# Decode attention plus gated MLP on one core: K turned by VectorE in 32x32 blocks instead of by TensorE

## The chip, the cores and the metric

One core of a Trainium2 chip runs the whole kernel. The time is that of one execution on the device, in microseconds (us); less is better. Engines: PE (TensorE) multiplies matrices and writes PSUM, DVE (VectorE) and ACT (ScalarE) work elementwise, POOL (GpSimd) fills constants, SP (SyncE) issues nearly all transfers. Transfers run on 16 DMA engines beside them. All data is float32.

## The reference, cut to what matters

```
xn  = layernorm(x)                          # x: 2 x 1 x 512
q   = xn @ wq                               # 32 heads of 128, 8 K/V heads (4 query heads share one)
k,v = the last 4096 positions of the caches # per batch row and K/V head: 4096 x 128
p   = softmax(q k^T / sqrt(128));  o = p v
out = x + o @ wo + ((relu(gate) * up) @ W_down),  gate = xn @ W_gate, up = xn @ W_up
```

Two batch rows, one new token each. K and V of the window are 2 x 8 x 4096 x 128 floats, 32 MB each; the weights are wq 8 MB, wo 8 MB and three of 3.5 MB. Every byte is used once, so some 95 MB have to come in.

## The kernel before

The K/V heads are taken in four groups g (a half of the heads, r, of one batch row, b: g = 2r + b), each of four K/V heads in two halves a of two heads. A load is one half's K or V: 4 MB, as 128 partitions of 8192 floats. Partition 2y + h holds positions 64y to 64y+63 of head h. That is 64 tiles of 128 x 128, with the head's 128 components along the free axis.

All large loads go through one ring of four slots (`ring`, `RING = 4`), all on SP's queue, in this order: wq in two parts, W_gate, W_up, then K(0,0), K(0,1), K(1,0), V(0,0), K(1,1), V(0,1), K(2,0), V(1,0) and so on up to K(3,1), V(2,1), then V(3,0), V(3,1), W_down, wo for r = 0, wo for r = 1 in five pieces. A load can be issued when the slot four loads before it has been read. The schedule is manual: on each engine the instructions run in the order of the program text.

After layernorm and the query projection (`q_ps`, L198), the queries are transposed and put into `qz`, a tile of zeros with 32 columns per slot, so that a score matmul writes 32 rows of PSUM. The gate and up projections follow (L225).

For each K half the work is `kwork(g, a, ...)`: per part s1 (0, 1), `transposes` turns 32 tiles of 128 x 128 on PE with an identity (L256), four into one PSUM bank `pk`, and `evacuate` copies each bank into `kT` in SBUF, by ACT and DVE in turn (L245), sorting the two heads apart. `scores` (L269) multiplies `qz` with a finished `kT` into the PSUM tile `s` (32 rows for each of four quarters, 512 positions wide). The scores of one part are issued behind the transposes of the next (`pend`).

`softmax(g)` runs in steps between the transposes of group g+1: maximum `m` (L278), its transpose `mt`, a maximum over the rows of a head `mx`, the negated scaled maximum `mb`, a matmul that gives it back to the partitions (`nm`), the exponential `p` with every value written twice (L302), eight PE transposes `pp` (L313) and two products with the mask `own` into `pt` (L314), sums `lp` and reciprocal `rl`.

`values(g, a, v)` (L333) multiplies `pt` with V into `o`, and then masks it by `own_u` into `on` (L339); `gather` (L350) adds rows by a matmul with `pick`; `finish` (L360, L361) sums and divides; `spread_heads(r)` (L366) brings a half of the heads into `oT`, the layout for wo. At the end `project_wide` (L430) multiplies W_down and most of wo into `yw`, and `project` (L434) the last four row blocks of wo.

The matmul of float32 appears as two records in the profile, so 16 score matmuls of a K half are 32 records.

Of the kernel before, what the change touches and what calls it, by code (L numbers as in the profile page):

```python
# [20 lines left out]
def kernel(  # L21
# [24 lines left out]
    Q = 4  # L46
# [64 lines left out]
    NSLOT = C * S1  # L111
# [10 lines left out]
    spread = const.tile([HR, NE, HR, NE], F32, name="spread")  # L122
    nc.gpsimd.memset(spread, 0.0)
    for e in range(NE):
        nc.gpsimd.tensor_copy(spread[:, e, :, e], ident[0:HR, 0:HR])
# [18 lines left out]
    by_h = const.tile([P, NP, HK], F32, name="by_h")  # L144
    nc.vector.tensor_reduce(
        out=by_h, in_=ident.rearrange("p (q a s k) -> p a k q s", q=Q, a=NP, s=S1), op=ALU.add, axis=AX.XY
    )

    half_of = const.tile([P, 2], F32, name="half_of")
    nc.vector.tensor_reduce(  # L150
        out=half_of, in_=ident.rearrange("p (y h) -> p h y", h=2), op=ALU.add, axis=AX.X
    )
    own = const.tile([P, 2, REP], F32, name="own")
    nc.vector.tensor_copy(own, half_of[:, :, None].to_broadcast([P, 2, REP]))

# [18 lines left out]
    xn = const.tile([B, D], F32, name="xn")  # L174
# [29 lines left out]
    for r in range(R):  # L204
        qs = work.tile([P, 512], F32, name=f"qs{r}", tag="qs")
        (nc.vector.tensor_copy if r else nc.scalar.copy)(qs, q_ps[r])
        qt = ps_kt.tile([P, REP, C, 16, B], F32, name=f"qt{r}", tag="kt")
        for i in range(REP):
            nc.tensor.transpose(  # L209
                qt[:, i].rearrange("p c s b -> p (c s b)"), qs[:, i * P:(i + 1) * P], ident  # L210
            )
        for b in range(B):
            dst = qz[:, r * B + b].rearrange("p (a s h k) -> p a s h k", a=NP, s=S1, h=2)
            for h in range(2):
                nc.vector.tensor_copy(  # L215
                    dst[:, :, :, h, 0:REP], qt[:, :, h::2, 0:S1, b].rearrange("p i a s -> p a s i")
                )

# [12 lines left out]
    gr = work.tile([P, FQ], F32, name="gr", tag="gr", bufs=1)  # L231
# [7 lines left out]
    HW = W // S1  # L239
    ss, pts, rls = {}, {}, {}  # L240
    kts, osb = {}, {}
    turn = [0]

    def evacuate(dst, src):
        (nc.vector.tensor_copy if turn[0] % 2 else nc.scalar.copy)(dst, src)  # L245
        turn[0] += 1

    def transposes(g, a, s1, kt_in):

        kt = ktp.tile([P, 2, HW], F32, name=f"kT{g}_{a}_{s1}", tag="kT")  # L250
        kts[g, a, s1] = kt
        for n in range(2 * Q):
            pk = ps_kt.tile([P, 512], F32, name=f"pk{g}_{a}_{s1}_{n}", tag="kt")
            for u in range(4):
                j = 8 * Q * s1 + 4 * n + u
                nc.tensor.transpose(pk[:, u * P:(u + 1) * P], kt_in[:, j * P:(j + 1) * P], ident)  # L256
            evacuate(
                kt[:, :, n * 256:(n + 1) * 256], pk.rearrange("p (y h) -> p h y", h=2),
            )
            yield  # L260

    def scores(g, a, s1):
        if (a, s1) == (0, 0):
            ss[g] = ps_s.tile([P, 512], F32, name=f"s{g}", tag="s")
        kt = kts.pop((g, a, s1))
        for h in range(2):
            n = (a * S1 + s1) * 2 + h
            for q in range(Q):
                nc.tensor.matmul(  # L269
                    ss[g][32 * q:32 * q + 32, :], qz[:, g, 32 * n:32 * n + 32],  # L270
                    kt[:, h, q * 512:(q + 1) * 512],
                    start=(a == 0 and s1 == 0 and h == 0), stop=(a == NP - 1 and s1 == S1 - 1 and h == 1),
                )

    def softmax(g):
# [3 lines left out]
        yield  # L279
        mt = ps_1.tile([1, P], F32, name=f"mt{g}", tag="misc")  # L280
        nc.tensor.transpose(mt, m, ident)
        mx = work.tile([1, NP, HK], F32, name=f"mx{g}", tag="mx")
        nc.vector.tensor_reduce(
            out=mx, in_=mt.rearrange("p (q a s k) -> p a k q s", q=Q, a=NP, s=S1), op=ALU.max, axis=AX.XY
        )
        mb = work.tile([1, NP, S1, HK], F32, name=f"mb{g}", tag="mb")
        nc.vector.tensor_scalar(
            mb, mx[:, :, None, :].to_broadcast([1, NP, S1, HK]), -SCALE, None, op0=ALU.mult
        )
        yield  # L290
        nm_ps = ps_1.tile([P, 1], F32, name=f"nm_ps{g}", tag="misc")
        for q in range(Q):
            nc.tensor.matmul(  # L293
                nm_ps[32 * q:32 * q + 32, :], mb.rearrange("p a s k -> p (a s k)"), ones, start=True, stop=True
            )
# [3 lines left out]
        p = work.tile([P, 512, 2], F32, name=f"p{g}", tag="p", bufs=1)  # L299
        l = work.tile([P, 1], F32, name=f"l{g}", tag="l")  # L300
        both = ss[g][:, :, None].to_broadcast([P, 512, 2])
        nc.scalar.activation(p, both, AF.Exp, bias=nm, scale=SCALE, accum_out=l)  # L302
        yield
        yield
        yield

        pts[g] = work.tile([P, 2, Q * NP * S1, 4, HK], F32, name=f"pt{g}", tag="pt")
        pv = p.rearrange("r y h -> r (y h)")
        for jh in range(2):
            pp = ps_kt.tile([P, 4, P], F32, name=f"pp{g}_{jh}", tag="kt")  # L310
            for u in range(4):
                lo = (4 * jh + u) * P
                nc.tensor.transpose(pp[:, u], pv[:, lo:lo + P], ident)  # L313
            nc.vector.tensor_tensor(  # L314
                pts[g][:, jh].rearrange("p n u k -> p u n k"), pp.rearrange("p u (n k) -> p u n k", k=HK),
                own.rearrange("p h i -> p (h i)")[:, None, None, :].to_broadcast([P, 4, Q * NP * S1, HK]), op=ALU.mult,
            )
            yield
        lp = ps_1.tile([HR, 1], F32, name=f"lp{g}", tag="misc")
        nc.tensor.matmul(lp, by_h.rearrange("p a k -> p (a k)"), l, start=True, stop=True)  # L320
# [3 lines left out]
    ons = {}  # L324

    def values(g, a, v):
        o = ps_1.tile([P, 512], F32, name=f"o{g}_{a}", tag=f"o{a}")
        for s1 in range(S1):
            for jh in range(2):
                for q in range(Q):  # L330
                    n = (q * NP + a) * S1 + s1
                    lo = (8 * Q * s1 + 8 * q + 4 * jh) * P
                    nc.tensor.matmul(  # L333
                        o[32 * q:32 * q + 32, :],
                        pts[g][:, jh, n].rearrange("p u k -> p (u k)"), v[:, lo:lo + 512],
                        start=(s1 == 0 and jh == 0), stop=(s1 == S1 - 1 and jh == 1),
                    )
        ons[a] = work.tile([P, 4, P], F32, name=f"on{g}_{a}", tag="on")
# [16 lines left out]
    def finish(g):  # L355
# [5 lines left out]
        nc.vector.tensor_scalar(osb[r][:, b], od, rls[g], 2.0, op0=ALU.mult, op1=ALU.mult)  # L361

    def spread_heads(r):
        op = ps_1.tile([P, NJ, B], F32, name=f"op{r}", tag="misc")
        for e in range(NE):
            nc.tensor.matmul(  # L366
                op, spread[:, e].rearrange("h k e -> h (k e)"),
# [5 lines left out]
    pend = []  # L373

    def kwork(g, a, kt_in, others=()):

        others = list(others)
        for s1 in range(S1):
            for n, _ in enumerate(transposes(g, a, s1, kt_in)):
                if n > 1 and others and next(others[0], "end") == "end":  # L380
                    others.pop(0)
                if (a, s1, n) == (0, 0, 1) and pend:
                    scores(*pend.pop())
            if pend:
                scores(*pend.pop())
# [107 lines left out]
```

## Time and profile before

| | |
|---|---|
| median of 3 runs | 231.82 us (231.73 to 232.03) |
| the profiled execution | 231.71 us; its span in the profile 229.9 us |
| PE, DVE, ACT, POOL busy | 182.2, 73.3, 46.6, 3.8 us |
| moved by DMA | 95.10 MB |
| mean granted clock of PE | 0.925 of full speed |

Busy time says how long an engine had instructions running, not whether anything waited for it. A line of the groups reads: line of the code, engine, operation, output and inputs, shapes, count, then busy time in us and mean ns of one, then the idle time just before them and what ended it. A line of the chain or of the timeline begins with start and length in us. A line of a stretch gives its length, the busy time of PE, PE's weight loads (PEld), DVE, ACT and POOL with counts, then PE's granted clock, the share of the DMA engines and GB/s.

### The profile page before, as it was taken

Reading aid. Unit: us, or ns where it says so; the run is one execution under the profiler, and the core shown is the slowest. Engines: PE = TensorE matmul, PEld = TensorE weight load, DVE = VectorE, ACT = ScalarE, POOL = GpSimd, SP = SyncE. Lnnn points to the kernel's source line nnn. Section 1 sums busy time; section 2 is a strip of 40 time slices with the busy share of each in tenths; the row PEclk is TensorE's granted clock in tenths of the full one; section 3 lists DMA queues with packets and bytes.
Section 4 is the critical chain, followed back from the end, with each engine's and each line's share of the span. In section 5 each row is a group of like instructions: output and inputs, shape, how many; then the busy total and the mean of one; then the engine's idle time right before and its main releaser. Section 6 shows DMA issues by size and latency. Waiting matters only on the chain.

```text
span 229.9 us, 3250 instructions
## 1 busy us (share of the span) xinstructions
PE 182.2 (79%) x1432; PEld 96.0 (42%) x1432; DVE 73.3 (32%) x143; ACT 46.6 (20%) x78; POOL 3.8 (2%) x17
## 2 busy tenths in 40 slices
PE   0483970819999889998899699589999965889493
PEld 0430230219666573661583563248566213124011
DVE  2400021024444561641572441247244144111000
ACT  2000100004444550440351340025134002000001
POOL 6000000000000000000000000000000000000000
PEclk9998598576999999999999999889999996799799
DMA  7999999999999999999999999999999999999980
GB/s 274 456 433 391 464 409 466 399 445 450 422 408 450 436 410 423 448 428 413 439 450 419 416 446 442 410 422 456 425 410 436 445 422 430 428 445 405 420 339 14
DMA packets 3921, 95.10 MB, mean 414 GB/s; under 512 B 442, under 2 KB 450, under 8 KB 836
## 3 DMA queue, kind: packets, MB, share of 16 engines
q1 hardware_dynamic: 3896, 94.90, 96.4%
q8 instruction: 11, 0.18, 0.3%
q14 instruction: 2, 0.02, 0.0%
q10 hardware_dynamic: 12, 0.01, 0.0%
HBM read 94.90 MB, written 0.00 MB: 413 GB/s over the span
## 4 chain that ended last, share of the span: by engine, by line
PE 51%; DMA 41%; DVE 4%; ACT 2%; issue 1%; SPq 1%
DMA k<-in_A_k_cache_dram 25%; PE pk L256 23%; PE s L269 11%; DMA wo<-in_A_wo_dram 10%; PE o L333 9%; DMA wq<-in_A_wq_dram 5%; PE q_ps L198 3%; PE pp L313 2%; ACT p L302 2%; PE oa L350 2%; DVE kT L245 1%; PE op L366 1%; SPq L449 1%; DVE on L339 1%; PE nm_ps L293 0%
## 5 line engine op out<-in xcount | busy, mean ns | idle before, releaser
L256 PE MATMUL pk<-ident,k 128*128 128x128 f32 x512 | 67.3, 286 | 8.4 <-DMA k<-in_A_k_cache_dram 8.4
L256 PEld LDWEIGHTS pk<-ident,k 128*128 128x128 f32 x512 | 57.7, 146 | 24.6 <-issue 21.0
L245 ACT COPY kT<-pk 128x512 f32<-128x512 f32 x64 | 37.5, 586 | 100.1 <-PE pk L256 100.1
L245 DVE COPY kT<-pk 128x512 f32<-128x512 f32 x64 | 44.2, 691 | 37.9 <-PE pk L256 37.8
L333 PE MATMUL o<-v,pt 128*32 128x512 f32 x256 | 34.2, 627 | 0.0
L269 PE MATMUL s<-kT,qz 128*32 128x512 f32 x256 | 32.1, 607 | 0.0
L339 DVE TENSOR_TENSOR on<-o,own_u 128x512 f32<-128x512 f32 x8 | 5.5, 692 | 39.4 <-PE o L333 39.4
L333 PEld LDWEIGHTS o<-v,pt 128*32 128x32 f32 x256 | 8.9, 114 | 20.0 <-issue 19.9
L198 PE MATMUL q_ps<-wq,xnT 128*32 128x512 f32 x64 | 12.3, 940 | 4.3 <-DMA wq<-in_A_wq_dram 4.3
L269 PEld LDWEIGHTS s<-kT,qz 128*32 128x32 f32 x256 | 7.0, 111 | 13.2 <-issue 13.2
L350 PE MATMUL oa<-on,pick 128*16 128x512 f32 x16 | 8.2, 596 | 4.2 <-DVE on L339 4.2
L430 PE MATMUL yw_ps<-wo,oT 128*2 128x512 f32 x56 | 7.9, 703 | 3.9 <-DMA wo<-in_A_wo_dram 3.9
L186 PE MATMUL xt_ps<-rep,xn 2*128 2x32 f32 x16 | 3.7, 402 | 8.7 <-DVE rep L179 8.7
L225 PE MATMUL u_ps<-wu,xnT 128*32 128x448 f32 x32 | 5.2, 816 | 6.6 <-DMA wu<-in_B_W_up_dram 6.6
L198 PEld LDWEIGHTS q_ps<-wq,xnT 128*32 128x32 f32 x64 | 2.9, 163 | 12.9 <-issue 7.6
L313 PE MATMUL pp<-ident,p 128*128 128x128 f32 x32 | 5.5, 306 | 2.4 <-ACT p L302 1.5
L455 ACT COPY yw<-yw_ps 128x512 f32<-128x512 f32 x1 | 0.6, 586 | 33.3 <-PE yw_ps L430 33.3
L186 PEld LDWEIGHTS xt_ps<-rep,xn 2*128 2x128 f32 x16 | 3.6, 319 | 8.7 <-DVE rep L179 8.7
L302 ACT ACTIVATE p<-s,nm 128x1024 f32<-128x1024 f32 x4 | 4.5, 1115 | 13.0 <-DVE nm L297 12.9
L314 DVE TENSOR_TENSOR pt<-pp,own 128x512 f32<-128x512 f32 x8 | 5.5, 692 | 3.8 <-PE pp L313 3.7
L215 DVE COPY qz<-qt 128x16 f32<-128x16 f32 x8 | 0.8, 167 | 17.6 <-PE qt L209 17.6
L225 PEld LDWEIGHTS u_ps<-wu,xnT 128*32 128x32 f32 x32 | 1.3, 160 | 10.5 <-DMA wu<-in_B_W_up_dram 7.4
(72 smaller groups left out, 60.9 us busy)
## 6 DMA issues: line engine op xcount, KB each, us to landing
k<-in_A_k_cache_dram SPq DMA_DIRECT2D x8, 4096.0 KB, 29.1
v<-in_A_v_cache_dram SPq DMA_DIRECT2D x8, 4096.0 KB, 29.0
wq<-in_A_wq_dram SPq DMA_DIRECT2D x2, 4096.0 KB, 16.9
wo<-in_A_wo_dram SPq DMA_DIRECT2D x1, 4096.0 KB, 31.7
wg<-in_B_W_gate_dram SPq DMA_DIRECT2D x1, 3584.0 KB, 29.6
wu<-in_B_W_up_dram SPq DMA_DIRECT2D x1, 3584.0 KB
wd<-in_B_W_down_dram SPq DMA_DIRECT2D x1, 3584.0 KB
wo<-in_A_wo_dram SPq DMA_DIRECT2D x1, 2048.0 KB, 20.7
```

The source lines that it names most:

```text
L186: nc.tensor.matmul(xt_ps[:, v, kc, :], lhsT, rep16.rearrange("r s b -> r (s b)"), start=True, stop=True)
L198: nc.tensor.matmul(q_ps[r][32 * c:32 * c + 32, :], xnT[:, 0, kc, :], wqt[kc // 2][:, kc % 2, n * 512:(n + 1) * 512], start=(kc == 0), stop ...
L225: nc.tensor.matmul(dst[32 * c:32 * c + 32, :], xnT[:, 1, kc, :], wt[:, kc, c * FQ:(c + 1) * FQ], start=(kc == 0), stop=(kc == KC - 1),)
L245: (nc.vector.tensor_copy if turn[0] % 2 else nc.scalar.copy)(dst, src)
L256: nc.tensor.transpose(pk[:, u * P:(u + 1) * P], kt_in[:, j * P:(j + 1) * P], ident)
L269: nc.tensor.matmul(ss[g][32 * q:32 * q + 32, :], qz[:, g, 32 * n:32 * n + 32], kt[:, h, q * 512:(q + 1) * 512], start=(a == 0 and s1 == 0 ...
L302: nc.scalar.activation(p, both, AF.Exp, bias=nm, scale=SCALE, accum_out=l)
L313: nc.tensor.transpose(pp[:, u], pv[:, lo:lo + P], ident)
L333: nc.tensor.matmul(o[32 * q:32 * q + 32, :], pts[g][:, jh, n].rearrange("p u k -> p (u k)"), v[:, lo:lo + 512], start=(s1 == 0 and jh == 0 ...
L339: nc.vector.tensor_tensor(ons[a], o.rearrange("p (u d) -> p u d", u=4), own_u[:, :, None].to_broadcast([P, 4, P]), op=ALU.mult)
L350: nc.tensor.matmul(oa[g].rearrange("h u d -> h (u d)"), pick[:, 8 - 8 * a:24 - 8 * a], ons[a].rearrange("p u d -> p (u d)"), start=(a == 0 ...
L430: nc.tensor.matmul(yw_ps[32 * c:32 * c + B, :], lhsT, w, start=(n < Q), stop=(n >= wide - Q))
```

## The change

K is no longer turned by PE. `keys(g, a, kt_in, between)` takes the two halves mh of the head's components (64 of 128). For each, DVE turns 32 x 32 blocks straight from the ring's slot in SBUF into `kt` in SBUF, four instructions of 128 x 1024 (`CUT = 4`). Afterwards partition 32x + i holds component i of a block of 32 components, for the positions that belong to the partitions 32x to 32x+31 before; the free axis runs over position, block and those 32 partitions. Score matmuls contract over all 128 partitions with a block-diagonal `qz` (32 columns: 4 blocks x, 2 halves a, 4 query heads), take every second column (`h::2`) and add up the four blocks of components. Their number stays 16 per K half.

`between` holds steps that run after the first half's scores: the gather of the half before, and for a = 0 also `finish` of the group before and, once, `spread_heads`.

`softmax(g)` follows the scores at once. The exponential is written by two instructions of 64 partitions into `pz`, a tile of 32 columns per position of which the rest are zero. `turn(g)`, behind the values of group g-1, transposes `pz` by DVE (128 x 1024) and copies it in sixteen pieces of 32 partitions, by ACT and DVE in turn, into `pt`. The mask of `o` is a step of its own, `mask`, behind `turn`. The constants `half_of` and `own` go, `by_h` is built in two parts, `spread` is a smaller tile read in shifted windows with one copy instead of eight, and the factor 2.0 in `finish` goes. The copies into `qz` become 32, of 32 partitions each, by ACT and DVE in turn. `xn` and `gr` are written in place; `yw` shares a buffer with `on`.

```diff
-    qz = const.tile([P, NG, NSLOT * 36], F32, name="qz")
+    JS = J // S1
+    NB = DH // 32
+    qz = const.tile([P, NG, NB, NP, 2, 32], F32, name="qz")
     nc.gpsimd.memset(qz, 0.0)
+    pz = const.tile([P, JS, 32], F32, name="pz")
+    nc.gpsimd.memset(pz, 0.0)
...
-        for b in range(B):
-            dst = qz[:, r * B + b].rearrange("p (a s h k) -> p a s h k", a=NP, s=S1, h=2)
-            for h in range(2):
-                nc.vector.tensor_copy(
-                    dst[:, :, :, h, 0:REP], qt[:, :, h::2, 0:S1, b].rearrange("p i a s -> p a s i")
+        for m in range(NB):
+            src = qt[32 * m:32 * m + 32, :, :, 0].rearrange("p i (t h) b -> p b t h i", h=2)
+            for x in range(Q):
+                d = qz[32 * x:32 * x + 32, r * B:r * B + B, m]
...
+                (nc.vector.tensor_copy if x % 2 else nc.scalar.copy)(dst, src)
...
-    def transposes(g, a, s1, kt_in):
...
-                nc.tensor.transpose(pk[:, u * P:(u + 1) * P], kt_in[:, j * P:(j + 1) * P], ident)
-            evacuate(
-                kt[:, :, n * 256:(n + 1) * 256], pk.rearrange("p (y h) -> p h y", h=2),
-            )
-            yield
...
+    CUT = 4
+
+    def keys(g, a, kt_in, between=()):
+
+        if a == 0:
             ss[g] = ps_s.tile([P, 512], F32, name=f"s{g}", tag="s")
...
+        for mh in range(2):
+            kt = ktp.tile([P, J, 2, 32], F32, name=f"kT{g}_{a}_{mh}", tag="kT")
+            src = kt_in.rearrange("p (j d) -> p j d", d=DH)[:, :, PK * mh:PK * mh + PK]
+            n = J // CUT
+            for c in range(CUT):
+                nc.vector.transpose(
+                    kt[:, c * n:(c + 1) * n].rearrange("p j m i -> p j (m i)"), src[:, c * n:(c + 1) * n]
                 )
+            for m in range(2):
+                for h in range(2):
+                    for s1 in range(S1):
+                        q = 2 * h + s1
+                        nc.tensor.matmul(
+                            ss[g][32 * q:32 * q + 32, :], qz[:, g, 2 * mh + m, a, h], kt[:, JS * s1:JS * s1 + JS, m, h::2],
+                            start=(a == 0 and mh == 0 and m == 0), stop=(a == NP - 1 and mh == 1 and m == 1),
+                        )
+            if mh == 0:
+                for step in between:
+                    step()
...
-        nc.scalar.activation(p, both, AF.Exp, bias=nm, scale=SCALE, accum_out=l)
...
+        pv = pz.rearrange("p j (i h) -> p j i h", h=2)
+        for h in range(2):
+            o = slice(PK * h, PK * h + PK)
+            nc.scalar.activation(
+                pv[o, :, :, h], ss[g][o].rearrange("p (j i) -> p j i", j=JS), AF.Exp, bias=nm[o], scale=SCALE, accum_out=l[o],
             )
...
+    def turn(g):
+        pT = work.tile([P, JS, Q, NP, REP], F32, name=f"pT{g}", tag="pT", bufs=1)
+        nc.vector.transpose(pT.rearrange("p j x t k -> p (j x t k)"), pz.rearrange("p j s -> p (j s)"))
+        pts[g] = work.tile([P, NP, S1, JS, 2, REP], F32, name=f"pt{g}", tag="pt")
+        n = 0
+        for h in range(2):
+            for s1 in range(S1):
+                q = 32 * (2 * h + s1)
+                for x in range(Q):
+                    (nc.vector.tensor_copy if n % 2 else nc.scalar.copy)(
+                        pts[g][32 * x:32 * x + 32, :, s1, :, h], pT[q:q + 32, :, x].rearrange("p j t k -> p t j k")
+                    )
+                    n += 1
...
     for a in range(NP):
-        kwork(0, a, load_kv(k_cache, "k", 0, a))
+        keys(0, a, load_kv(k_cache, "k", 0, a))
+    softmax(0)
+    turn(0)
+    late = []
     for g in range(1, NG):
         for a in range(NP):
             kt_in = load_kv(k_cache, "k", g, a)
             v_in = load_kv(v_cache, "v", g - 1, a)
-            kwork(g, a, kt_in, [softmax(g - 1)] if a == 0 else [])
+            keys(g, a, kt_in, late)
             if a:
-                gather(g - 1, a - 1)
-            elif g % B == 1 and g > 1:
-                spread_heads((g - 2) // B)
+                softmax(g)
             values(g - 1, a, v_in)
-        gather(g - 1, NP - 1)
-        finish(g - 1)
+            if a:
+                turn(g)
+            mask(g - 1, a)
+            late = [lambda g=g, a=a: gather(g - 1, a)]
+            if a:
+                late.append(lambda g=g: finish(g - 1))
+                if g % B == 0:
+                    late.append(lambda g=g: spread_heads((g - 1) // B))
+    for step in late:
+        step()
```

More of the change, by code (lines that the diff above doesn't have):

```diff
@@ L120 @@
     oT = const.tile([P, R, NJ, B], F32, name="oT")
[L122 removed]
+    spread = const.tile([HR, HR + 1, NE], F32, name="spread")
     nc.gpsimd.memset(spread, 0.0)
[L124 to L125 removed]
+    nc.gpsimd.tensor_copy(spread[:, 0:HR, NE - 1], ident[0:HR, 0:HR])
     pick = const.tile([P, 24], F32, name="pick")
@@ L262, in scores @@
-    def scores(g, a, s1):
-        if (a, s1) == (0, 0):
-            ss[g] = ps_s.tile([P, 512], F32, name=f"s{g}", tag="s")
[L265 to L272, printed above, removed]
-                )
+    osb = {}
@@ L275, in softmax @@
+    ls = {}
     def softmax(g):
@@ L308, in softmax @@
[L308 to L316, printed above, removed]
-            )
-            yield
+        l = ls[g] = work.tile([P, 1], F32, name=f"l{g}", tag="l")
```

98 lines of the change are left out of this document (29 added, 69 removed).

## The prediction

> **What bounds the kernel now.** I read the page from the top: the busy shares, the transfers, the chain of work that ended last, the groups; then stretches of time, and the order of events at the end.
>
> ```profile
> span 229.9 us, 3250 instructions
> PE 182.2 (79%) x1432; PEld 96.0 (42%) x1432; DVE 73.3 (32%) x143; ACT 46.6 (20%) x78; POOL 3.8 (2%) x17
> DMA  7999999999999999999999999999999999999980
> 5.00:220.00 215.00, 176.31 (x1360) 94.66 (x1364) 72.40 (x139) 44.74 (x76) 0.00 (x0) 0.92 1.00 430
> 19.16 31.70 DMA k<-in_A_k_cache_dram
> 121.52 26.47 DMA k<-in_A_k_cache_dram
> ```
>
> PE is the busiest engine, yet the transfers set the time: their engines are busy in every slice but the first and last, and between 5 and 220 us their share is 1.00 at 430 GB/s. The first K block lands at 19.16 + 31.70 = 50.86 us; K of group 3, half a=0, ten loads of 4 MB later in the order of issue, at 121.52 + 26.47 = 147.99: 9.71 us a load. So K and V of one group, four loads, come every 38.85 us, and each K block was issued 26 to 32 us before it landed: the queue is about three loads deep. Whatever the engines do costs nothing until they free ring slots too late, or until the work behind the last K block runs past the landing of wo.
>
> The end, in order of time (the column after the start is the length):
>
> ```profile
> 193.41 0.69 DVE pt L314
> 195.01 5.52 PE o L333 x32
> 213.00 0.19 DVE L371 COPY oT<-op 128x32 f32<-128x32 f32 x1 [4.34 <-PE op L366]
> 216.35 6.90 PE L430 MATMUL yw_ps<-wo,oT 128*2 128x512 f32 x48 [3.39 <-DMA wo<-in_A_wo_dram]
> 223.78 1.04 PE L430 MATMUL yw_ps<-wo,oT 128*2 128x512 f32 x8 [0.52 <-DMA wo<-in_A_wo_dram]
> ```
>
> The weights of the last group, which I call pt3, are ready at 194.10. The rest of the attention is over at 213.19, 19.09 us later, and PE then waits for wo until 216.35. So pt3 has only 3.2 us to spare. That is the number the change is measured against.
>
> **What is removed and what replaces it.**
>
> ```profile
> L256 PE MATMUL pk<-ident,k 128*128 128x128 f32 x512 | 67.3, 286 | 8.4 <-DMA k<-in_A_k_cache_dram 8.4
> L245 ACT COPY kT<-pk 128x512 f32<-128x512 f32 x64 | 37.5, 586 | 100.1 <-PE pk L256 100.1
> L245 DVE COPY kT<-pk 128x512 f32<-128x512 f32 x64 | 44.2, 691 | 37.9 <-PE pk L256 37.8
> L235 DVE STREAM_TRANSPOSE hT<-hh 128x448 f32<-128x448 f32 x1 | 0.9, 936 | 0.0
> L190 DVE COPY xnT<-xt_ps 128x256 f32<-128x256 f32 x1 | 0.4, 425 | 3.8 <-PE xt_ps L186 3.8
> 4.76 0.28 DVE L134 TENSOR_REDUCE own_u<-ident 128x4 f32<-128x128 f32 x1
> 4.96 0.36 DVE L138 TENSOR_REDUCE fold<-ident 128x32 f32<-128x128 f32 x1
> ```
>
> Gone are 512 PE transposes (67.3 us) and 128 evacuations (37.5 us of ACT, 44.2 of DVE). New are 64 DVE transposes of 128x1024. Their price is the main term. The one transpose in the trace took 936 ns for 448 elements, 2.09 ns each; but it reads single words 14 apart, while the new ones read runs of 64 words. Two contiguous copies (256 elements 425 ns, 512 elements 691) give 1.04 ns an element and 159 ns fixed. What a scattered read costs is seen in two reductions of the same 128 elements: 0.28 us where words lie in runs of 8, 0.36 where they lie 32 apart, 0.65 ns an element more. Then 448 x (1.04 + 0.65) + 159 = 916 ns, 2% under the 936 measured: the transpose itself costs one element's time. So 1024 x 1.04 + 159 = 1.22 us; from below I know no row of this operation. Bounds: 936/448 x 1024 = 2.14 us if its rate is what it is, and 1.22 if the stride explains it; I take 1.22, by the sum that meets the row. Back to back they overlap: fold starts 0.20 us after own_u, which lasts 0.28. I take 1.14 from start to start, a half of a K block (four) 4.64 us, a whole one 9.2.
>
> The Trainium skill, "Vector Engine (DVE) Microarchitecture Reference", section 3.8, states that the transpose sustains one element per cycle and lane, as this row suggests once its stride is taken off. Against the overlap stands "VectorE: DVE Perf Modes", section "The DRAIN you can't avoid": the next operation does not start until the pipeline is empty. By it each transpose would cost 0.08 us more and the sum below would end about 4 us later, near 242; the two rows above contradict it here, so it gets no chance beyond the range.
>
> **The loop that decides.** VectorE takes its work in program order, and now three of its steps wait for PE inside each group: the division of the group before (it waits for the first half's scores and a gather), the maximum (for the second half's scores), and the mask (for the values). In that time no K is turned. Before, K was turned by PE and evacuated in small steps, and none of this stood in its way. The rows for the steps:
>
> ```profile
> 101.45 1.85 PE s L269 x16
> 165.31 3.57 PE o L333 x32
> 163.41 1.90 PE op L366 x16
> 108.41 1.03 PE oa L350 x2
> 107.67 0.70 DVE on L339
> 186.47 0.68 DVE L360 TENSOR_REDUCE od<-oa 16x128 f32<-16x512 f32 x1 [1.12 <-PE oa L350]
> 187.18 0.28 DVE L361 TENSOR_SCALAR osb<-od,rl 16x128 f32<-16x128 f32 x1
> 188.23 0.70 DVE m L278
> 190.40 1.22 ACT p L302 x2
> L215 DVE COPY qz<-qt 128x16 f32<-128x16 f32 x8 | 0.8, 167 | 17.6 <-PE qt L209 17.6
> L175 DVE TENSOR_SCALAR xn<-xc,rs 2x512 f32<-2x512 f32 x1 | 0.5, 475 | 0.0
> L322 DVE RECIPROCAL rl<-lp 16x1 f32<-16x1 f32 x4 | 0.6, 146 | 0.0
> 41.19 5.18 PE L225 MATMUL u_ps<-wu,xnT 128*32 128x448 f32 x32 [6.60 <-DMA wu<-in_B_W_up_dram]
> ```
>
> The number of score matmuls stays (16 records a half, 1.85 us); their new operand steps by two words, which no row prices: nothing at best, double at worst (another 1.85 a half); I take nothing, since each column of these matmuls takes PE longer than reading one word. From the maximum to the exponential, 188.23 to 190.40: 2.17 us. The exponential becomes two of half the partitions, 512 elements each; the old one takes 1.22 for 1024, a 512-element ACT copy 0.59, so 2 x 0.8 = 1.6. "turn" is one transpose (1.22) and sixteen copies of 32x256, eight on ACT beside eight on DVE. A DVE copy lies between 0.17 (16 elements) and 0.48 (512), I take 0.30 for its 256; an ACT one under 0.59 (512 elements), I take 0.37. So DVE is through with turn after 1.22 + 8 x 0.30 + 0.15 for the reciprocal = 3.8, and `pt` is whole after 1.22 + 8 x 0.37 = 4.2. Before, this was eight PE transposes and two products, done between pieces of K.
>
> PE's clock enters here. With its transposes gone PE idles while DVE turns the next half, 4.64 us and more:
>
> ```profile
> 20.00:21.00 1.00, 0.00 (x0) 0.00 (x0) 0.00 (x0) 0.00 (x0) 0.00 (x0) 1.00 0.91 393
> 22.00:23.00 1.00, 0.27 (x4) 0.20 (x8) 0.00 (x0) 0.00 (x0) 0.00 (x0) 0.50 0.93 401
> 27.00:28.00 1.00, 1.00 (x12) 0.34 (x8) 0.00 (x0) 0.00 (x0) 0.00 (x0) 0.50 1.06 459
> 28.00:29.00 1.00, 1.00 (x13) 0.09 (x5) 0.00 (x0) 0.59 (x1) 0.00 (x0) 0.93 1.06 459
> ```
>
> After about 2 us of idling the granted clock (third column from the right) is 0.50, and it takes 5 us of work to return. The values at 195.01 took 5.52 us for the 3.57 of 165.31 in the same way. So I take the scores that follow an idle half at half clock, 3.5, a gather 1.5, and values behind such scores 4.5.
>
> The sum, as times at which VectorE is through. Group 0: K lands 50.9, turned 60.1; second block lands 60.6, turned 69.8; scores 71.6; to the exponential 73.8; 75.4; turn 79.2. The next K has been there since 70.3, so from here VectorE runs without a pause.
> - Group 1, a=0: 9.2 + 1.85 + 3.5 + 0.7 = 15.3, to 94.5. Its a=1: 9.2 + 0.3 (first scores and gather just outlast the second half) + 1.85 + 2.17 + 1.6 + 3.8 + 0.7 = 19.6, to 114.1.
> - Group 2, a=0, now with the division: 4.64 + 3.5 + 1.5 + 1.0 + 4.64 + 3.5 + 4.5 + 0.7 = 24.0, to 138.1; a=1 19.6, to 157.7.
> - Group 3, a=0: 24.0 + 2.1 (the spreading of the heads, 1.90 and a copy), to 183.8; a=1 without its mask 18.9: DVE has done its part of pt3 at 202.7 instead of 194.10 (ACT at 203.1, still ahead of its use).
>
> A group takes 43.6 us against 38.85 of transfers. The ring just holds: K of group 3, a=0, is read by 175.1 and its slot is wanted by the stream at 147.99 + 3 x 9.71 = 177.1, so no transfer starts late; 2 us more and the stream begins to pause.
>
> The end: the last mask, gather and division of group 2 now stand behind pt3, 0.70 + 1.03 + 1.0 and hops, 2.8. Then the old 19.09: oT at 202.7 + 21.9 = 224.6, past 216.35. PE goes on without idling, 48 records at 0.11 us to 229.9, the last 8 to 230.8, where before the last wide product ended at 224.82. That is 6.0 us later; the output follows as before. Break-even lies at pt3 = 196.7.
>
> **What costs nothing, and its cover.** The 32 small copies into qz (16 ACT, 16 DVE, some 0.2 us each) fall behind the query projection, ahead of the up projection, for which wu lands only at 41.19, and K comes at 50.86; without that cover they would cost 3 us. POOL writes larger zero tiles but a smaller spread, and one copy for eight; its results are first wanted by DVE's set-up, ahead of the landing of wq, and a fraction of a microsecond there hides behind 20 us of queued transfers. SP's queue keeps its order; what it waits for is now DVE's last read of a K block instead of PE's. The 2.0 that left the division costs nothing either way.
>
> **The profiled execution** took 231.71 us (1.8 more than its span), 0.1 under the median of 231.82. 231.71 + 6.0 = 237.7.
>
> **Rivals.**
> - Hidden anyway, no change, 231.7. If PE keeps its clock in the gaps, a=0 of groups 2 and 3 costs 4.64 + 1.85 + 1.03 + 1.0 + 4.64 + 1.85 + 3.57 + 0.7 = 19.3 and 21.4, its a=1 19.3, and pt3 comes at 192.4, before 196.7. For it: transfers are saturated, so that wo's landing then sets the end. Against: the idle gaps of 4.64 us. It decides as soon as 6 us are saved anywhere on the loop, of which cheaper copies or an earlier clock could give some. Chance 0.28.
> - The transpose or the stepped operand is dear. Every 0.1 us on a transpose is 6.8 us over 68 of them. At 2.14 us it is 1.0 x 68 = 68 later, near 305; if the 936 hold a fixed cost (936 - 448 x 1.04 = 470 ns), 1.54 us each, 0.32 x 68 = 22 later, near 259. Stepped operands at half speed: nine exposed halves at 1.85 more, near 254. For it, only that nothing here shows these forms; against it, the stride sum that met 936. Chance 0.13.
> - Faster: transfers speed up when PE and ACT leave SBUF alone.
>
> ```profile
> 125.00:130.00 5.00, 3.09 (x32) 1.56 (x21) 0.85 (x2) 0.59 (x1) 0.00 (x0) 1.00 1.04 442
> 155.00:160.00 5.00, 4.95 (x42) 4.23 (x42) 3.90 (x7) 2.85 (x5) 0.00 (x0) 1.00 0.97 419
> 135.00:140.00 5.00, 5.00 (x49) 3.33 (x50) 2.77 (x4) 2.35 (x4) 0.00 (x0) 1.00 1.04 446
> 195.00:200.00 5.00, 5.00 (x33) 1.17 (x32) 0.00 (x0) 0.00 (x0) 0.00 (x0) 0.62 0.98 418
> ```
>
> The first two speak for it: 442 GB/s with few copies, 419 with many. At 442 throughout, 215 x (1 - 430/442) = 5.8 us less, 226. The other two are against: 446 with many copies, 418 with none. And VectorE's loop would then set the end all the same. Chance 0.09.
>
> **How the numbers follow.** My case, pt3 late by some microseconds, has 0.50. Its own range: a clock that returns early in each burst and copies at their lower bounds (8 x 0.13 less in each of four turns, 4 us) give 232.2 and up; a clock that returns later, at 2 us more for each of three groups, and the pauses of the stream that then begin, about 245. With 0.2% (0.46 us, about what this measurement can tell from no change) on each side of 231.7: slower 0.50 + 0.13, same 0.28, faster 0.09. The range reaches from 231.2 to 246, leaving out the faster case and most of the dear one.
>
> **What would show it.** Right: transposes of 1.1 to 1.25 us, 64 of them; PE 110 to 130 us busy, at a clock well under 0.92; DVE waiting on PE before the division, the maximum and the mask; pt's last copy near 203; PE not waiting for the first wo. Wrong: wo's landing at 216 still awaited by PE (then 231.7), transposes over 1.3 us, DMA shares under 0.95 before 215 us (ring slots late), or a rate above 435 GB/s.

## The result and the profile after

The changed kernel takes 234.53 us (median of 4 runs, 233.47 to 235.69), the kernel before, run beside it, 231.93 (4 runs, 231.73 to 232.20): a ratio of 1.0113, 95% interval 1.0063 to 1.0162. So the change costs 2.6 us; forecast were 6.0 (237.7). Ratios, here and below, leave out executions more than 1.5% above the fastest of their kernel, while medians count all. The profiled execution took 235.69 us, the slowest of the four, 4.0 more than the profiled one of before.

The page of the changed kernel: busy shares, the instruction queue of the DMA engines, and two groups (busy time, mean ns of one, idle time ahead). Then the long stretch that was shown of before.

```profile
span 233.7 us, 2113 instructions
PE 145.3 (62%) x864; PEld 40.0 (17%) x864; DVE 113.4 (49%) x178; ACT 26.6 (11%) x70; POOL 3.7 (2%) x11
...
q8 instruction: 6, 0.10, 0.2%
...
L252 DVE STREAM_TRANSPOSE kT<-k 128x1024 f32<-128x1024 f32 x64 | 73.2, 1207 | 5.5 <-DMA k<-in_A_k_cache_dram 5.5
...
L292 ACT ACT_TABLE_LOAD x1 | 1.3, 1283 | 33.2 <-DVE nm L286 33.2
```

```profile
5.00:220.00 215.00, 135.22 (x751) 35.81 (x752) 112.19 (x172) 24.78 (x68) 0.00 (x0) 0.81 1.00 430
```

The transposes take 1.207 us each, as forecast. Transfers still run at share 1.00 and 430 GB/s up to 220 us. PE has lost 37 us of work and a good part of its clock (0.81, before 0.92).

The timeline of VectorE in the changed kernel, cut to the end of group 0, to half a=0 of groups 2 and 3, and to the end (start, length, engine and line; in brackets the idle time ahead and what ended it):

```profile
80.73 0.15 DVE L312 RECIPROCAL rl<-lp 16x1 f32<-16x1 f32 x1
...
115.33 0.69 DVE L332 TENSOR_TENSOR on<-o,own_u 128x512 f32<-128x512 f32 x1
115.94 4.61 DVE L252 STREAM_TRANSPOSE kT<-k 128x1024 f32<-128x1024 f32 x4
124.31 0.68 DVE L353 TENSOR_REDUCE od<-oa 16x128 f32<-16x512 f32 x1 [3.76 <-PE oa L343]
...
125.23 4.60 DVE L252 STREAM_TRANSPOSE kT<-k 128x1024 f32<-128x1024 f32 x4
135.98 0.69 DVE L332 TENSOR_TENSOR on<-o,own_u 128x512 f32<-128x512 f32 x1 [6.15 <-PE o L323]
...
179.39 0.69 DVE L332 TENSOR_TENSOR on<-o,own_u 128x512 f32<-128x512 f32 x1 [6.88 <-PE o L323]
...
198.99 0.15 DVE L312 RECIPROCAL rl<-lp 16x1 f32<-16x1 f32 x1
...
201.83 0.68 DVE L353 TENSOR_REDUCE od<-oa 16x128 f32<-16x512 f32 x1 [1.98 <-PE oa L343]
...
222.70 0.19 DVE L364 COPY oT<-op 128x32 f32<-128x32 f32 x1 [4.34 <-PE op L359]
230.39 0.29 DVE L443 COPY yo<-y_ps 128x128 f32<-128x128 f32 x1 [7.50 <-PE y_ps L415]
```

VectorE's own pieces have the forecast lengths. What differs are the waits for PE: 3.76 where 5.0 was put (scores 3.5 and gather 1.5), 6.15 and 6.88 where 8.0 was put (scores 3.5, values 4.5). So pt3 came at 199.14, not at 202.7. The same stretch on PE, and then PE at the end:

```profile
118.35 1.92 PE L259 MATMUL s<-kT,qz 128*32 128x512 f32 x2 [3.54 <-DVE kT L252]
120.61 2.78 PE L259 MATMUL s<-kT,qz 128*32 128x512 f32 x11 [0.34 <-DVE kT L252]
122.34 1.05 PE L343 MATMUL oa<-on,pick 128*16 128x512 f32 x1
123.17 1.07 PE L259 MATMUL s<-kT,qz 128*32 128x512 f32 x3
...
203.60 6.58 PE L323 MATMUL o<-v,pt 128*32 128x512 f32 x32
...
222.59 6.19 PE L411 MATMUL yw_ps<-wo,oT 128*2 128x512 f32 x56
```

The half is turned at 120.55, but PE starts at 118.35: the first of its eight score products needs positions of two of the four pieces only. The second waits for the whole half, and the rest follows from 120.61. No line waits for wo any more; the wide product follows oT at once. Three stretches of the changed kernel show the clock (third column from the right): the first burst, the values of group 1, and the first values of the last group:

```profile
118.00:123.00 5.00, 4.31 (x14) 0.75 (x18) 2.55 (x3) 0.00 (x0) 0.00 (x0) 0.50 0.99 426
131.00:137.00 6.00, 4.91 (x42) 1.70 (x34) 1.02 (x2) 0.00 (x0) 0.00 (x0) 1.00 0.99 426
204.00:209.00 5.00, 5.00 (x28) 1.18 (x24) 0.00 (x0) 0.00 (x0) 0.00 (x0) 0.50 0.97 419
```

### The profile page after: what moved, and what is told of

Same layout as the page of the kernel before. It is cut to its first block, busy times and chain, and to the rows that moved or that the text cites. A ratio compares the mean times of both kernels' runs of the same rounds, so it can differ in the third digit from the quotient of the medians.

```text
span 233.7 us, 2113 instructions
## 1 busy us (share of the span) xinstructions
PE 145.3 (62%) x864; PEld 40.0 (17%) x864; DVE 113.4 (49%) x178; ACT 26.6 (11%) x70; POOL 3.7 (2%) x11
## 4 chain that ended last, share of the span: by engine, by line
DVE 37%; PE 33%; DMA 22%; ACT 4%; issue 2%; SPq 0%; ACTq 0%; DVEq 0%
DVE kT L252 25%; DMA k<-in_A_k_cache_dram 13%; PE s L259 11%; PE o L323 9%; DMA wq<-in_A_wq_dram 9%; PE yw_ps L411 4%; DVE pt L305 4%; PE q_ps L195 3%; ACT pz L292 3%; DVE pT L298 2%; DVE on L332 2%; PE oa L343 2%; PE op L359 2%; DVE m L272 1%; DVE od L353 1%
## 5 line engine op out<-in xcount | busy, mean ns | idle before, releaser
L259 PE MATMUL s<-kT,qz 128*32 128x512 f32 x256 | 64.3, 807 | 50.5 <-DVE kT L252 50.5
L252 DVE STREAM_TRANSPOSE kT<-k 128x1024 f32<-128x1024 f32 x64 | 73.2, 1207 | 5.5 <-DMA k<-in_A_k_cache_dram 5.5
L292 ACT ACTIVATE pz<-s,nm 64x512 f32<-64x512 f32 x8 | 5.8, 729 | 99.6 <-DVE nm L286 99.5
L343 PE MATMUL oa<-on,pick 128*16 128x512 f32 x16 | 12.2, 859 | 4.6 <-DVE on L332 4.6
L305 ACT COPY pt<-pT 32x256 f32<-32x256 f32 x32 | 12.8, 402 | 5.6 <-DVE pT L298 5.2
L305 DVE COPY pt<-pT 32x256 f32<-32x256 f32 x32 | 9.1, 285 | 0.5
L298 DVE STREAM_TRANSPOSE pT<-pz 128x1024 f32<-128x1024 f32 x4 | 5.0, 1246 | 8.3 <-ACT pz L292 8.3
L183 PE MATMUL xt_ps<-rep,xc 2*128 2x32 f32 x16 | 3.7, 402 | 8.4 <-DVE rep L176 8.4
L225 PE MATMUL g_ps<-wg,xnT 128*32 128x448 f32 x32 | 5.0, 788 | 0.0
L359 PE MATMUL op<-osb,spread 16*128 16x32 f32 x32 | 3.9, 273 | 1.1 <-DVE osb L354 1.1
```

The lines of the kernel that those rows point to most:

```text
L183: nc.tensor.matmul(xt_ps[:, v, kc, :], lhsT, rep16.rearrange("r s b -> r (s b)"), start=True, stop=True)
L252: nc.vector.transpose(kt[:, c * n:(c + 1) * n].rearrange("p j m i -> p j (m i)"), src[:, c * n:(c + 1) * n])
L259: nc.tensor.matmul(ss[g][32 * q:32 * q + 32, :], qz[:, g, 2 * mh + m, a, h], kt[:, JS * s1:JS * s1 + JS, m, h::2], start=(a == 0 and mh == ...
L292: nc.scalar.activation(pv[o, :, :, h], ss[g][o].rearrange("p (j i) -> p j i", j=JS), AF.Exp, bias=nm[o], scale=SCALE, accum_out=l[o],)
L298: nc.vector.transpose(pT.rearrange("p j x t k -> p (j x t k)"), pz.rearrange("p j s -> p (j s)"))
L305: (nc.vector.tensor_copy if n % 2 else nc.scalar.copy)(pts[g][32 * x:32 * x + 32, :, s1, :, h], pT[q:q + 32, :, x].rearrange("p j t k -> p ...
```

## The experiments

The theory: transfers set the time as long as pt3 comes before 196.7, and VectorE's loop now makes it later, by the waits for PE in half a=0 of groups 2 and 3, where PE also runs at half clock. Rivals: the half clock alone, wherever the waits lie; the stepped operand `h::2`; the fixed cost of many short transposes.

**e1: the division taken off the first half.** `finish(g - 1)` goes behind both halves of K, `spread_heads` behind the mask; nothing is saved but the wait.

```diff
-    late = []
+    late, fin = [], []
...
             keys(g, a, kt_in, late)
+            if fin:
+                fin.pop()()
...
             mask(g - 1, a)
+            if a == 0 and g > 1 and g % B == 1:
+                spread_heads((g - 2) // B)
...
-                late.append(lambda g=g: finish(g - 1))
+                fin.append(lambda g=g: finish(g - 1))
```

> The division of the group before (finish) is moved from between the two halves of K to behind the second half, and the spreading of the heads behind the mask, so that VectorE turns both halves without waiting for PE. Loop theory (VectorE waiting for PE between the halves makes pt3 late, and pt3 sets the end): the a=0 blocks of groups 2 and 3 fall from 20.7 and 23.6 us to about 15.5, pt3 comes near 187 (K of group 3, a=1, lands only at 167), PE waits for wo again, and the time is that of the kernel before within 0.3%. Rival, that transfers or ring slots set the end: no change, 234 to 235.

It took 230.73 us (5 runs, 230.52 to 230.82) against 231.74: ratio 0.9953 (0.9942 to 0.9965), faster than both kernels, and below the kernel before by a little more than the 0.3% expected (e6 has the reason). VectorE's timeline in e1, and PE's line of the wide product:

```profile
116.34 0.69 DVE L332 TENSOR_TENSOR on<-o,own_u 128x512 f32<-128x512 f32 x1
...
125.98 0.64 DVE L353 TENSOR_REDUCE od<-oa 16x128 f32<-16x512 f32 x1
...
131.65 0.69 DVE L332 TENSOR_TENSOR on<-o,own_u 128x512 f32<-128x512 f32 x1 [4.72 <-PE o L323]
...
188.08 0.69 DVE L332 TENSOR_TENSOR on<-o,own_u 128x512 f32<-128x512 f32 x1
```

```profile
215.28 8.41 PE L413 MATMUL yw_ps<-wo,oT 128*2 128x512 f32 x56 [4.22 <-DMA wo<-in_A_wo_dram]
```

The block of group 2 lasts 15.3 us instead of 20.65, pt3 comes at 188.08, and PE waits for wo again. All of this at a mean clock of 0.806, lower than in the changed kernel (0.824). So a low clock costs nothing by itself here; it costs where VectorE waits for PE inside the loop.

**e3: PE kept busy.** Unneeded matmuls behind the first half's scores and behind the values (they write a tile that nobody reads) hold the clock at 0.90.

```diff
+    def fill(n):
+        for _ in range(n):
+            nc.tensor.matmul(junk, ident, qz[:, 0].rearrange("p m a h k -> p (m a h k)"), start=True, stop=True)
...
+                fill(3)        # behind the scores and steps of the first half
...
+            fill(4)            # behind mask
```

> PE gets extra matmuls whose results nobody reads: three of 128x512 behind the first half's scores and four behind each values, so that it doesn't idle. Clock theory (the half clock after each idle half is what makes scores and values long): granted clock near 1.0 from 60 us on, a half's scores 1.9 us everywhere, the a=0 blocks of groups 2 and 3 near 18.5 and 21, values ahead of the end 3.6 instead of 6.6; pt3 near 194 and the time 231.7 to 232.5. Rival, that the waiting itself and not its clock matters: blocks within 0.5 us of before, 234 or later.

231.42 us (12 runs, 230.23 to 234.85), ratio 0.9978 (0.9959 to 0.9997). VectorE's timeline in e3:

```profile
97.94 0.69 DVE L341 TENSOR_TENSOR on<-o,own_u 128x512 f32<-128x512 f32 x1 [7.79 <-PE o L332]
...
118.03 0.69 DVE L341 TENSOR_TENSOR on<-o,own_u 128x512 f32<-128x512 f32 x1
...
125.44 0.68 DVE L362 TENSOR_REDUCE od<-oa 16x128 f32<-16x512 f32 x1 [2.19 <-PE oa L352]
...
136.53 0.69 DVE L341 TENSOR_TENSOR on<-o,own_u 128x512 f32<-128x512 f32 x1 [5.58 <-PE o L332]
...
197.33 0.69 DVE L341 TENSOR_TENSOR on<-o,own_u 128x512 f32<-128x512 f32 x1
```

The wait for the gather falls from 3.76 to 2.19. Half a=0 of group 2 takes 18.5 us instead of 20.65 (118.72 to 137.22), that of group 3 20.7 instead of 23.6: together 5.0 us less, as expected of the clock. But pt3 came at 197.3, not near 194, since the other blocks took 3.2 us more, 2.2 of it in half a=0 of group 1: there the mask waits 7.79, against 5.63 in the changed kernel, for values that stand behind the extra matmuls. So pt3 falls by 1.8 us only, and the end takes 29.5 us from pt3 to the output copy instead of 31.2, with the values at full clock. Together that is 3.5 us between the two profiled executions (232.22 and 235.69), nearly the whole loss of the change. e1 and e3 are two sides of one cause: the waits inside the loop, made longer by the clock.

**e5: the changed kernel again,** as a ground for the small experiments, on another chip.

> The changed kernel once more. Its four runs lay 2.2 us apart, those of the kernel before 0.5 us. If the granted clock after each idle half makes the difference from run to run, this trace shows the same transposes to 0.05 us, but scores and values behind the idle halves of other lengths, and the end moves by as much as pt3 moves against 199.1. Rival, that the spread comes from the transfers: K landings move by as much as the end. Time 233.5 to 235.7.

235.17 us (5 runs, 234.73 to 235.98) against 231.71, ratio 1.0150 (1.0132 to 1.0168). VectorE's timeline in e5, the lines that answer to 124.31, 135.98 and 201.83 above, and the stretch in which the values of group 1 run:

```profile
124.53 0.68 DVE L353 TENSOR_REDUCE od<-oa 16x128 f32<-16x512 f32 x1 [3.29 <-PE oa L343]
...
137.40 0.69 DVE L332 TENSOR_TENSOR on<-o,own_u 128x512 f32<-128x512 f32 x1 [7.35 <-PE o L323]
...
201.37 0.68 DVE L353 TENSOR_REDUCE od<-oa 16x128 f32<-16x512 f32 x1 [1.12 <-PE oa L343]
```

```profile
131.00:137.00 6.00, 6.00 (x46) 1.44 (x38) 0.00 (x0) 0.00 (x0) 0.00 (x0) 0.75 1.02 437
```

The same program, and its waits move by 0.5 to 1.2 us in both directions: where a burst of PE meets the half clock differs from run to run. Behind the wait of 7.35 the clock was 0.75 from 131 to 137 us, where it was 1.00 in the changed kernel. The expectation that the end moves as pt3 does failed: pt3 came 0.4 us later than in the changed kernel, the output copy 0.5 us sooner (229.90), as the gather behind pt3 waited 1.12 us instead of 1.98. The Trainium skill, "TensorE: Matmul & The Clock Gate", Part 1, says that the clock is judged over a window of some 3.4 us that runs freely and does not start with the kernel. The runs fit, though none shows the window itself: those of before lie within 0.5 us, those of the changed kernel within 2.2, and in the changed kernel the last part of the path goes through PE's short bursts.

**e2: one transpose per half (`CUT = 1`).** It saves fixed costs of VectorE.

```diff
-    CUT = 4
+    CUT = 1
```

> Each half of K is turned by one instruction of 128x4096 instead of four of 128x1024 (CUT 1). Per half three fixed costs of some 0.07 us go. Loop theory: a K block takes 8.8 instead of 9.13 us, pt3 comes 2.5 us earlier, and the end 2 to 2.5 us earlier, 232 to 232.5. Rival, that VectorE's time is hidden beside the transfers: no change, 234 to 235.

The expectation failed: 242.41 us (239.97 to 244.44), ratio 1.0407 (1.0363 to 1.0451). A half of a K block did fall from 4.61 to 4.44 us. PE and VectorE in e2, and a stretch of its transfers:

```profile
116.22 4.44 DVE L252 STREAM_TRANSPOSE kT<-k 128x4096 f32<-128x4096 f32 x1
120.72 3.64 PE L259 MATMUL s<-kT,qz 128*32 128x512 f32 x16 [7.32 <-DVE kT L252]
124.13 1.29 PE L343 MATMUL oa<-on,pick 128*16 128x512 f32 x2
125.46 0.68 DVE L353 TENSOR_REDUCE od<-oa 16x128 f32<-16x512 f32 x1 [4.80 <-PE oa L343]
...
138.28 0.69 DVE L332 TENSOR_TENSOR on<-o,own_u 128x512 f32<-128x512 f32 x1 [7.47 <-PE o L323]
...
203.21 0.69 DVE L332 TENSOR_TENSOR on<-o,own_u 128x512 f32<-128x512 f32 x1
```

```profile
175.00:180.00 5.00, 3.44 (x20) 0.92 (x24) 1.51 (x1) 0.00 (x0) 0.00 (x0) 0.57 0.63 229
```

Now all 16 score records stand behind the whole half, and the gather begins only as they end, where in the changed kernel its records lie among the last scores (122.34 and 123.19). The waits are 4.80 and 7.47, nearly the 5.0 and 8.0 of the prediction. That pt3 comes at 203.2, close to the 202.7 forecast for the kernel of four pieces, is in part luck: group 0 ended 2.5 us later than forecast, and the two blocks took 22.7 and 24.9 us, not 24.0 and 26.1. K of group 3, half a=0, is read by 176.5, 1.4 us later than the prediction had it, and the stream pauses (share 0.63); it had put the first pause at 2 us more.

**e11 and e12: one transpose per half, with PE kept busy** as in e3. Does one long transpose lose by the clock alone?

> One instruction per half (CUT 1) with the extra matmuls that keep PE busy, whose results nobody reads. If the harm of one cut comes through the half clock (16 score records that start late take 3.6 instead of 1.9 us): division's wait near 2.9 us instead of 4.8, no pause in the transfers, 231 to 233. If it has another cause: 238 and more.

> The same kernel as e11: one transpose a half, and unneeded matmuls behind the values and the first half's scores that keep PE's clock up. The profile of e11 cannot be read, its granted clock being 0.571 throughout, while its timed runs at clocks of 0.89 to 0.90 took 233.7 to 239.0. Open: does one long transpose a half (242.4 without the extra matmuls) lose by PE's half clock alone, or also by PE starting late? By clock alone the wait for the gather in group 2, half a=0, would be that of four cuts kept warm, 2.19 us, and pt of group 3 near 197. By the late start, all 16 score records stand behind the transpose even at full clock: gather wait 1.9 + 1.0 + 0.4 = 3.3 us or more, mask wait 1.9 + 3.6 + 0.4 = 5.9 or more, pt of group 3 near 199 to 202, time 233 to 239.

The profile of e11 can't be used: PE's granted clock was 0.571 on average, 0.55 to 0.59 in each third, and that execution took 302 us; its other runs, at clocks of 0.89 to 0.90, lay between 233.7 and 239.0. e12, the same kernel in one more run, took 234.05 us at a clock of 0.897. VectorE in e12:

```profile
126.06 0.68 DVE L362 TENSOR_REDUCE od<-oa 16x128 f32<-16x512 f32 x1 [2.99 <-PE oa L352]
...
167.35 0.68 DVE L362 TENSOR_REDUCE od<-oa 16x128 f32<-16x512 f32 x1 [4.63 <-PE oa L352]
...
201.27 0.69 DVE L341 TENSOR_TENSOR on<-o,own_u 128x512 f32<-128x512 f32 x1
```

In group 2 the clock is full in both (1.00 from 118 to 127 us), and the wait is 2.99 against 2.19 with four pieces: 0.8 us for the late start alone, a little less than expected. The mask's wait is the same, 5.62 against 5.58: at full clock the late start costs only ahead of the gather. In group 3 the clock fell in spite of the extra matmuls (0.82 from 158 to 167 us, where e3 had 1.00), and the gather's wait was 4.63. So both count: pt3 at 201.27 lies between 197.33 (four pieces, warm) and 203.21 (one piece, not warm). How much of the rest is the clock, one run can't say.

**e9: two transposes per half (`CUT = 2`).**

> Each half of K in two instructions of 128x2048 (CUT 2). One instruction (CUT 1) saved 0.36 us a K block on VectorE, as expected, and yet cost 8 us. If that was because PE then can't begin with the first score matmul (positions of the first half of the tile) while VectorE still turns the rest, two cuts keep that start and save 0.24 us a block: first records of each half before its last transposes end, wait of the division near 3.8 us, time 233 to 235. Rival, that long transposes are themselves the harm: between 4 cuts and 1, 237 to 239.

232.47 us (12 runs, 230.20 to 235.41), ratio 0.9989 (0.9957 to 1.0022), a little better than expected. A K block takes 8.89 us instead of 9.13, 1.9 us over eight blocks; the waits for the gather, 3.37 and 3.28, are those of four pieces, since the first scores still start at the half of the transposes; pt3 came at 197.65. Longer transposes as such do no harm. The spread of 5.2 us fits a kernel that sits near break-even, where the clock decides: its fastest runs, 230.2, are as fast as e10 below, which waits for wo. Only one of its runs was traced, so this is not shown.

**e4 and e8: the operand in runs.** The score products read 16 neighbouring columns instead of every second one, which sorts columns wrongly between the two heads.

```diff
-  kt[:, JS * s1:JS * s1 + JS, m, h::2]
+  kt[:, JS * s1:JS * s1 + JS, m, 16 * h:16 * h + 16]
```

> The score matmuls read runs of 16 columns instead of every second one; the positions are then sorted wrongly between the two heads, the number of operations is the same. If the stepped operand costs nothing, as I took it: a half's scores 2.0 us at full clock as now, and the time 234 to 235. If it is dear: scores near 1.85 or less and the time 1 us or more below.

> The kernel with the score operand in runs of 16 columns once more, beside the changed kernel on the same chip; its scores take the wrong columns, with the same number of operations. If stepping by two words costs nothing: within 0.5 us of the changed kernel, and bursts of scores at full clock within 0.1 us of its own. If it costs what separated the two before: 1.4 us below it.

233.17 and 233.23 us, ratios 1.0066 (1.0045 to 1.0088) and 1.0057 (1.0036 to 1.0077): about 1.9 us better than e5. One execution of e4 took 644 us, which nothing here explains; the others lay between 231.90 and 234.26. PE at the same place at full clock, first the changed kernel, then e8:

```profile
69.73 2.01 PE L259 MATMUL s<-kT,qz 128*32 128x512 f32 x14 [1.20 <-DVE kT L252]
```

```profile
69.70 1.92 PE L259 MATMUL s<-kT,qz 128*32 128x512 f32 x14 [1.21 <-DVE kT L252]
```

The step of two words costs 0.09 us of 2.01 here, where the prediction put nothing and feared 1.85. At half clock there is no difference (eleven records take 2.78 us in the changed kernel at 141.26 and in e4 at 140.83). The nine exposed halves that the prediction counted give 0.8 us; the other 1.1 us lies in bursts that met another clock, and whether the shorter bursts cause that is not settled.

**e7: the table of the exponential loaded early,** by one exponential of a single element behind the projections.

```diff
+    early = const.tile([1, 1], F32, name="early")
+    nc.scalar.activation(early, ones, AF.Exp)
```

> The changed kernel with one exponential of one element ahead of the K loop, so that ACT's table load (1.28 us, which the first softmax now waits for) falls into idle time. Loop theory: everything behind the first softmax comes 1.3 us earlier, pt3 near 197.9, the end 1.3 us earlier, 233.2 against 234.5, the clock's spread aside. Rival, that the transfers set the end: no change.

234.19 us (233.25 to 234.75), ratio 1.0099 (1.0080 to 1.0119), 1.0 below e5. VectorE in e7:

```profile
79.52 0.15 DVE L314 RECIPROCAL rl<-lp 16x1 f32<-16x1 f32 x1
...
197.67 0.15 DVE L314 RECIPROCAL rl<-lp 16x1 f32<-16x1 f32 x1
...
229.07 0.29 DVE L445 COPY yo<-y_ps 128x128 f32<-128x128 f32 x1 [7.50 <-PE y_ps L417]
```

Against the changed kernel the first reciprocal comes 1.21 us sooner, the last 1.32, the output copy 1.32: the load of 1.283 us was exposed, and past break-even the end follows pt3 one to one, as the prediction had it.

**e6: e1 with as many instructions as before.** 280 matmuls of one element (1,120 instructions) that nobody reads, to see why wo lands earlier in e1 (215.28) than before (216.35).

> The kernel with the division behind the keys (the first of these runs, 230.7) with 280 more matmuls of one element on PE, in its idle stretches, whose result nobody reads: 1120 instructions, about what the change took away from PE. Theory of the instruction stream (fewer instructions to fetch leave one DMA engine less to do, so the last piece of wo lands 1.1 us earlier than in the kernel before): 11 instruction packets instead of 7, last landing near 226.2, time 231.6 to 231.9. Rival (an earlier issue of wo, or another cause): time 230.5 to 230.9 as without them.

232.12 us (231.77 to 232.47), ratio 1.0016 (1.0007 to 1.0024). The instruction queue in the page of e1:

```profile
q8 instruction: 7, 0.11, 0.2%
```

The same line of e6, which is also that of before, and e6's wait for wo:

```profile
q8 instruction: 11, 0.18, 0.3%
...
216.29 8.93 PE L421 MATMUL yw_ps<-wo,oT 128*2 128x512 f32 x56 [4.21 <-DMA wo<-in_A_wo_dram]
```

wo lands 1.0 us later with the instructions back. An earlier issue is not the cause: the first piece of wo was issued at 185.90 in e1 and at 185.35 in e6. So e1's gain over the kernel before is that PE's 1,100 instructions are not fetched over the same DMA engines. The Trainium skill, "Runtime: NRT & Kernel Launch", section "Instruction fetch mechanics", has an engine refill its instructions by DMA in blocks of 16 KiB, 256 instructions, at a cost that is mostly hidden. The size agrees (four packets more for 1,120 instructions, 0.11 MB in seven). Hidden it is not here, beside a stream that keeps the DMA engines full. Nor do the bytes explain it (0.07 MB is 0.16 us at 430 GB/s). By the same line the eleven packets took 0.3% of 16 engines' time, so about 1 us each on one engine, an estimate: four more are 4 us on a single engine, or 0.3 us spread over all sixteen. On which engines they ran the page doesn't say, so what makes it 1.0 us is open. The other 0.4 us of e6 is PE at half clock in the wide product, 8.93 us against 8.41.

**e10: e1 with the early table and two pieces.**

> Division behind the keys, table load early, two cuts: all that the earlier runs showed to take from VectorE's loop. pt3 near 186 or earlier, but K of group 3, a=1, lands at 167 and wo's landing sets the end: 230.5 to 230.9, no faster than the division alone (230.7).

230.21 us (5 runs, 230.14 to 230.51) against 231.68, ratio 0.9939 (0.9927 to 0.9951): the lowest of all, though its interval overlaps that of e1. VectorE and PE in e10:

```profile
167.39 8.89 DVE L254 STREAM_TRANSPOSE kT<-k 128x2048 f32<-128x2048 f32 x4 [1.81 <-DMA k<-in_A_k_cache_dram]
...
214.80 6.88 PE L415 MATMUL yw_ps<-wo,oT 128*2 128x512 f32 x48 [4.22 <-DMA wo<-in_A_wo_dram]
```

VectorE waits for K and PE for wo: the transfers alone set this time.

## Why the prediction was wrong in size

**Right:** the direction and the path. Transposes 1.207 us each (1.22 forecast), 9.13 a K block (9.2), reciprocal 3.82 us after the start of turn in group 0 (3.8), transfers unmoved at 430 GB/s, no wait for wo, the one-to-one rule behind break-even (e7), the pause of the stream when K is read later (e2), the half clock in the gaps. The overlap held too: four transposes of 1.207 us take 4.61, so each starts some 0.07 us before the one ahead of it has ended. The rule that the prediction set against it has an exception: the Trainium skill, "VectorE: DVE Perf Modes", section "The DRAIN you can't avoid", also says that the next instruction starts earlier if it is not held. Where break-even lies no run shows; e9, with pt3 at 197.6, still took no longer than the kernel before.

**The mis-sized term:** "24.0" for half a=0 of group 2 and "24.0 + 2.1" for that of group 3. They measured 20.65 (116.02 to 136.67) and 23.6. The sentence that failed is "I take the scores that follow an idle half at half clock, 3.5, a gather 1.5, and values behind such scores 4.5", laid one behind the other and behind the turned half. Two things shorten it. The half comes in four pieces, and PE begins with the first scores at 118.35, 2.2 us before the half is done, so that the gather runs among the last of them: 3.76 where e2, which starts late, has 4.80 and the prediction 5.0. And the clock comes back inside the scores and values (1.00 in 131 to 137 us): 6.15 and 6.88, where e5, whose clock came back later, and e2 have 7.35 and 7.47 and the prediction 8.0. e2 is the kernel that the sentence described. This term takes 5.9 us from the sum.

**Missed, the other way:** the table load of 1.28 us ahead of the first exponential (VectorE was through with group 0 at 80.88, not 79.2), and 1.85 us at the end, where oT came 23.75 us after pt3 and not 21.9: the gather behind pt3 and the values after it ran at half clock (1.98 us for the gather's wait, 6.58 for the values where 5.52 was taken over from before). The other blocks add some 1.0 us to pt3, and the wide product was 0.3 shorter than put.

The sum for the profiled execution: 6.0 - 5.9 + 1.3 + 1.0 + 1.85 - 0.3 = 4.0, as measured against the profiled run of before. So that the forecast had the right sign is in part luck: with the two blocks as they were, its own terms leave 0.1 us, and nearly all of the measured cost lies in what it had missed. The median is 1.2 us below the profiled execution. That fits waits that differ from run to run, as in e5, but the other three runs were not traced; one sum from one clock pattern could not say it, and a range for the clock was put only on the groups, not on the runs.

**The rivals.** The dear transpose and a dear stepped operand are out (1.207 us; 0.09 us a half). Faster transfers: none in this kernel, but e1 and e10 show a gain of that sign from another source, fewer instruction fetches. "Hidden anyway" priced the two blocks at a kept clock well: 19.3 and 21.4, and e3 has 18.5 and 20.7. In the changed kernel the clock was not kept. It also named what would decide for it, 6 us off the loop: e1 takes the division's wait away and gets there.

## What to carry to other kernels

When work moves to an engine that also holds steps waiting for others, cost the waits between the pieces, not the work: here the moved work was priced within 2%, and one division that waited inside the loop decided the sign. Let the consumer start on the first pieces, and put a step that waits behind work that doesn't need it. A time that hangs on PE's short bursts spreads from run to run; take several profiles before believing a microsecond of it.

## What was not expected of the hardware

That instructions can be felt in a stream of transfers: some 1,100 PE instructions less, 4 packets, and the last weights were there 1.0 us earlier (e1 against e6 and against the kernel before). And that one program, on the same path, can meet waits of 6.15 or 7.35 us at the same place, as the changed kernel and e5 did, with the clock from 131 to 137 us at 1.00 in the one and 0.75 in the other.
